# Attention backward: transposes of dS, dK, dV and dQ all by DMA, and twelve products of a pair on GpSimd

## The chip, the cores and the metric

The kernel runs on one core of a Trainium2 chip. The metric is device time in microseconds, the median of three runs. The program orders the instructions of TensorE, SyncE and GpSimd by hand in the part that is changed here; ScalarE and VectorE follow the order of the code's emission through a scheduler. Engines are called PE (TensorE), ACT (ScalarE), DVE (VectorE), POOL (GpSimd) and SP (SyncE) in the profile.

## The reference

One transformer block with adaptive layer norm, forward and backward: sequence 2048, width 512, 32 heads of 16, and a squared-ReLU MLP of width 1792. The result is the block's output and the gradients of its nine differentiable inputs.

```python
def _A_ref(x, wqkv, wo):
    ...
    scores = jnp.einsum('bhqd,bhkd->bhqk', q, k) * scale
    p = _softmax(scores, axis=-1)
    o = jnp.einsum('bhqk,bhkd->bhqd', p, v)
    ...
h = _layernorm(x, axis=-1) * (1 + ca) + sa
x = x + ga * _A_ref(h, A_wqkv, A_wo)
h = _layernorm(x, axis=-1) * (1 + cb) + sb
x = x + gb * _B_ref(h, B_w1, B_b1, B_w2, B_b2)
...
_out, _vjp = jax.vjp(_f, A_x, A_wqkv, A_wo, B_w1, B_b1, B_w2, B_b2, c, w_mod)
_grads = _vjp(grad_out)
```

The change lies in the backward pass of the attention: from stored Q, K, V and dO it makes, for each head, S = QK, P = exp(S), dP = dO V (with the correction term in two extra rows), dS = P * dP, and from these dV, dK (sums over queries) and dQ (a sum over keys).

## The kernel before, in words

The forward pass and the MLP's backward come first (to about 1173 us of the span), then attention backward (`attn_bwd`, to about 2380), then the gradients of the QKV projection.

Attention backward goes over 16 pairs of heads, `(g, jp)`: `g` counts eight groups of four heads, `jp` the two pairs in each. A pair has four chunks `c` of 512 keys and 16 blocks `ib` of 128 queries. Four blocks of queries in one chunk make a group; `m` counts the 16 groups of a pair, `m = 4c + ib // 4`. One step handles one `(c, ib)` for both heads `a` of the pair:

- TensorE makes S into PSUM tile `st` (line 1608), ScalarE its exponential into `pu` (line 1611).
- One step later, TensorE makes dP into PSUM tile `dp` (line 1522), and VectorE multiplies it by `pu` into `ds` (line 1526). For one product of a group, where `off(c, ib)` says so, ScalarE copies dP into SBUF instead (line 1540) and GpSimd multiplies (line 1541). `off` is true in ten of the 16 groups.
- Some steps later, `kv` adds dK and dV of both heads in `acckv` (line 1459); at the end of a chunk ScalarE scales it into `kvT` (line 1462).
- When a group's four steps have their `ds`, SyncE issues one DMA that transposes the group's 32 blocks of 128x128 into a buffer `dsT` (line 1549). Four buffers are called `dsT`; the fifth is the upper half of a large tile `keep` and carries its name in the profile. Where `no_turn` is false (four groups of 16, those with `ib // 4 == 0`), the first four blocks are turned on TensorE (line 1565) and copied by ScalarE (line 1566) instead, and the DMA does the other 28.
- Two groups' buffers together feed the products for dQ into `accq` (`dq`, line 1484), eight batches, two at each even step; the list `pendq` keeps them back until it holds more than eight, so that they run about two groups after the second transpose could be issued. At the end of a pair VectorE scales `accq` into `dqT` (line 1492).

`kvT` and `dqT` have the wrong orientation: heads' dimensions on partitions. They are put into `turnq`, and popped at the fourth step of a group (line 1603): `turn` turns eight blocks of `kvT` on TensorE (line 1472), and ScalarE writes dK and dV from PSUM into `dk_t` and `dv_t` (line 1476); `turn_q` does the same with four blocks of `dqT` (line 1500) and `dq_t` (line 1502). A pair has two turns of `kvT` and one of `dqT`. They borrow the three `st` buffers in PSUM.

GpSimd also issues the loads of the next pair and group of heads, spread over the groups (`pieces`, line 1597), each behind a one-element copy (`tick`, line 1596) that holds it back until the last group's `ds` has begun.

TensorE, SyncE and GpSimd run their instructions in the order of the code; a waiting instruction holds back all behind it on its engine.

Of the kernel before, what the change touches and what calls it, by code (L numbers as in the profile page):

```python
# [9 lines left out]
BF16 = mybir.dt.bfloat16  # L10
# [9 lines left out]
P = 128  # L20
DH = 16
# [84 lines left out]
class K:  # L106
# [1284 lines left out]
    def load_group(self, g):  # L1391
# [5 lines left out]
        if g < 2:  # L1397
            T, o = {}, 0
            for n, e in width.items():
                if g:  # L1400
                    T[n] = qp.tile([P, e], BF16, name=f"{n}g")[:]
                elif n == "K":
                    T[n] = self.keep[:, :e]
                else:
                    T[n] = self.q0[:, o:o + e]
                    o += e
            self.Tq[g] = T
        T, pieces = self.Tq[g % 2], []
        for n, (src, rows) in fm.items():
# [21 lines left out]
    def attn_bwd(self):  # L1431
# [7 lines left out]
        tc, nc = self.tc, self.nc  # L1439
        S, D, H, NQ, ST, SC = self.S, self.D, self.H, self.NQ, self.ST, self.SC  # L1440
        G = 4
        W = 4 * DH
        kvp, stp, dpp = self.kvp, self.stp, self.dpp
# [3 lines left out]
        nc.vector.memset(acckv[:], 0.0)  # L1447
        accq = accp.tile([P, 512], F32, name="accq")
        masked, kvs = self.masked, self.kvs
        pend, pendq, turnq, two = [], [], [], []  # L1450
        own = dT_free[-1]

        def kv(u):
            (T, g, jp, c, ib, kvT, pu, ds) = u
            for j, (n, src) in enumerate((("Q", ds), ("dO", pu))):
                for a in range(2):
                    r = 64 * j + 32 * a
                    col = (2 * jp + a) * DH
                    nc.tensor.matmul(acckv[r:r + DH, :], lhsT=T[n][:, ib, col:col + DH], rhs=src[:, a, :],  # L1459
                                     start=(ib == 0), stop=(ib == ST - 1))  # L1460
            if ib == ST - 1:
                nc.scalar.activation(kvT[:, 512 * c:512 * (c + 1)], acckv[:], ACT.Copy, scale=kvs[:])

        def turn(g, jp, kvT, s0):

            if kvT is None:
                return turn_q(g, jp)
            h0 = 4 * g + 2 * jp
            n = ST // 2
            tp = stp.tile([P, n, P], BF16, name="st")  # L1470
            for st in range(n):
                nc.tensor.transpose(tp[:, st, :], kvT[:, (s0 + st) * P:(s0 + st + 1) * P], self.ident[:])
            v = tp[:].rearrange("p s (t a e) -> p t s a e", t=2, a=2)
            for t, dst in enumerate((self.dk_t, self.dv_t)):
                d = dst[:, s0:s0 + n, h0 * DH:(h0 + 2) * DH].rearrange("p s (a d) -> p s a d", a=2)
                nc.scalar.copy(d, v[:, t, :, :, 0:DH])

        def dq(u):
# [12 lines left out]
            if (c, ib0) == (SC - 1, ST - 2 * G):  # L1491
                nc.vector.tensor_scalar(self.dqT[:], accq[:], self.scale, None, ALU.mult)
                turnq.append((g, jp, None, 0))

        def turn_q(g, jp):

            h0 = 4 * g + 2 * jp
            tp = stp.tile([P, ST // G, P], BF16, name="st")
            for b in range(ST // G):
                nc.tensor.transpose(tp[:, b, :], self.dqT[:, b * P:(b + 1) * P], self.ident[:])  # L1500
            for h in range(2):
                nc.scalar.copy(self.dq_t[:, 8 * h:8 * h + 8, h0 * DH:(h0 + 2) * DH].rearrange("p (s i) e -> p s i e", i=2),
                               tp[:, 2 * h:2 * h + 2, :].rearrange("p i (s e) -> p s i e", s=G))

        def kv_two(n=2):
            for _ in range(n):
                u = pend.pop(0)
                kv(u)
                (T, g, jp, c, ib, kvT, pu, ds) = u
                if ib < ST - 1:  # L1510
                    continue
                if c % 2 and (g, jp) == (NQ - 1, 1):
                    turnq.append((g, jp, kvT, 4 * (c - 1)))
                elif c == SC - 1:
                    turnq.extend((g, jp, kvT, s0) for s0 in (0, ST // 2))

        def dP(u, a):

# [9 lines left out]
        def odd(c, ib):  # L1528
            return (c * SC + ib // G) % 2 == 1

        def no_turn(c, ib):
            return ib // G > 0

        def off(c, ib):
            return odd(c, ib) or (c > 1 and ib // G == 2)

        def dP_pool(u, dp):
            (T, g, jp, c, ib, kvT, pu, dsg, i, grp) = u
            f = (self.junk6, self.csq)[(c * SC + ib // G) % 2]
            nc.scalar.copy(f[:], dp[:])  # L1540
            nc.gpsimd.tensor_tensor(dsg[:, i, 1], f[:], pu[:, 1, :], ALU.mult)  # L1541
# [26 lines left out]
        tick = self.tick  # L1568
        wmt = self.load_wmt()
        T = self.T0  # L1570
        last = None
        for g in range(NQ):
            for jp in range(2):
                if jp == 0:
                    if g + 1 < NQ:
                        Tn, later = self.load_group(g + 1)
                    else:
                        Tn, later = None, self.wq_pieces(1) + wmt[2 * g + 1:]
                    cut = len(later) // 2 if Tn else len(later)
                    pieces = self.pair_pieces(g, 1) + wmt[2 * g:2 * g + 1] + later[:cut]  # L1580
                    later = wmt[2 * g + 1:2 * g + 2] + later[cut:]
                elif g + 1 < NQ:
                    pieces = self.pair_pieces(g + 1, 0) + later
                else:
                    pieces = [(self.xhat1_6[:, st, :], self.xhat1_d.rearrange("(st p) d -> p st d", p=P)[:, st, :])
                              for st in range(ST)]
                kvT = kvp.tile([P, S], BF16, name="kvT")
                end = (g, jp) == (NQ - 1, 1)
                total = len(pieces)
                for c in range(SC):  # L1590
                    c0 = 512 * c
                    for ib0 in range(0, ST, G):
                        m = c * (ST // G) + ib0 // G
                        while pieces and ((total - len(pieces)) * SC * ST <= m * G * total or m == SC * ST // G - 1):
                            if last:
                                nc.gpsimd.tensor_copy(tick[:], last[7][0:1, 0, 0, 0:1])
                            nc.gpsimd.dma_start(*pieces.pop(0))
                        dsg, grp = self.dsp.tile([P, G, 2, 512], BF16, name="ds"), []
                        for i in range(G):
                            ib = ib0 + i  # L1600
                            q = slice(ib * P, (ib + 1) * P)
                            if turnq and i == 3 and m >= (7 if turnq[0][2] is None else 2):
                                turn(*turnq.pop(0))
                            pu = self.pup.tile([P, 2, 512], BF16, name="pu")
                            for a in range(2):
                                stt = stp.tile([P, 512], F32, name="st")
                                rs = slice(64 * jp, 64 * jp + 64)
                                nc.tensor.matmul(stt[:], lhsT=T["QT"][rs, q], rhs=masked["KT"][a][rs, c0:c0 + 512],  # L1608
                                                 start=True, stop=True)
                                held = dP(last, a) if last else None  # L1610
                                nc.scalar.activation(pu[:, a, :], stt[:], ACT.Exp, scale=self.scale)  # L1611
                                if held is not None:
                                    dP_pool(last, held)
                                if a == 0 and i % 2 == 1 and odd(c, ib) and len(pend) >= 4:
                                    kv_two(1)
                            if last:
                                dS(last)
                            last = (T, g, jp, c, ib, kvT, pu, dsg, i, grp)
                            if i % 2 == 1 and len(pend) >= 4:
                                kv_two(1 if odd(c, ib) else 2)  # L1620
                            elif i % 2 == 0 and len(pendq) > 2 * G:
                                for _ in range(4 if end else 2):
                                    dq(pendq.pop(0))
                            if i == 2:
                                turn_ds(dsg, grp, no_turn(c, ib), end and m > 2)
            T = Tn
        with tc.manual_schedule(engines=ALL):
# [23 lines left out]
            self.cs_bc(2)  # L1651
            turn(*turnq.pop(0))
            self.dw_mm(k1, 1, 1, 0, ST)
        assert not turnq and not pend
        self.dw_open = [(1, 0, k0), (2, 0, v0), (1, 1, k1)]

    def dw_mm(self, pt, t, kt, a, b):
# [308 lines left out]
```

## Time and profile before

| | us |
|---|---|
| median of three runs | 2506.41 |
| lowest, highest | 2501.06, 2510.86 |
| the profiled execution, first to last instruction | 2498.5 |
| attention backward in it, from the first transpose of dS | 1173 to about 2380 |

The profiled execution's own time is known only by this span; the median of the runs lies 7.9 us (0.3%) above it.

| engine | busy us in the whole span | share |
|---|---|---|
| PE | 2410.2 | 96% |
| ACT | 2283.1 | 91% |
| DVE | 1695.0 | 68% |
| POOL | 753.5 | 30% |

The shares are averages over parts of the program with different limits: DVE's 68% is made of about three to six tenths in the forward part and over nine tenths in attention backward. DMA transposes are issued on SP's queue (q1 in the profile, 344.68 MB, 1.25 million packets over the whole run), plain loads mostly on POOL's (q0, 104.04 MB). The time of a DMA instruction on SP's queue is that of issuing it; "to landing" is the time from the start of the issue to the completion of its data.

### The profile page before, as it was taken

To read this page: it belongs to the slowest core of one execution; us is meant where nothing else is said; L and a number is where in the kernel's file an instruction comes from. 1 tells how busy PE (TensorE), PEld (TensorE's weight loads), DVE (VectorE), ACT (ScalarE), POOL (GpSimd) and SP (SyncE) were. 2 spreads that over 40 slices of the span, in tenths; PEclk is the share of its full clock that TensorE was granted. 3 is DMA by queue.
4 is the path that set the end of the run, shared out by engine and by line. 5 is a ranking of instruction groups with operands and counts; after the bars stand their busy time and mean duration, and the time that the engine had idled before them with its cause. 6 is when DMAs were issued, how large, how long until landed. Compare 5 with 4: busy or idle time off the path is not lost.

```text
span 2498.5 us, 67897 instructions
## 1 busy us (share of the span) xinstructions
PE 2410.2 (96%) x26211; PEld 1061.6 (42%) x26439; DVE 1695.0 (68%) x3487; ACT 2283.1 (91%) x3757; POOL 753.5 (30%) x1337
## 2 busy tenths in 40 slices
PE   8999999999999999999999999999999999999998
PEld 4555555555555555583233332333333333333343
DVE  6222322422332343576999999999999999999957
ACT  7999999999999997534999999999999999999945
POOL 2344531220131022245222323322333222322223
PEclk9999999999999999999999999999999999999999
DMA  4589661541243045499999999999999999999997
GB/s 166 135 179 208 169 125 47 132 100 40 92 114 98 23 123 147 110 199 216 232 235 233 232 227 231 237 234 231 230 235 239 234 230 236 234 233 236 238 217 192
DMA packets 1293547, 454.13 MB, mean 182 GB/s; under 512 B 1236948, under 2 KB 1261398, under 8 KB 1293222
## 3 DMA queue, kind: packets, MB, share of 16 engines
q1 hardware_dynamic: 1252422, 344.68, 71.8%
q0 software_dynamic: 38720, 104.04, 13.9%
q8 instruction: 207, 3.39, 0.6%
q10 hardware_dynamic: 2080, 1.05, 0.2%
q14 instruction: 118, 0.97, 0.1%
HBM read 75.83 MB, written 64.49 MB: 56 GB/s over the span
## 4 chain that ended last, share of the span: by engine, by line
PE 49%; ACT 35%; DMA 7%; issue 5%; DVE 3%; POOL 1%; SPq 1%; ACTq 0%; DVEq 0%; POOLq 0%
ACT pu L391 26%; PE st L1608 17%; PE acckv L1459 8%; ACT pu L1611 6%; DMA dsT<-ds 5%; PE accq L1484 5%; PE st L388 4%; PE dp L1522 2%; PE accbank L322 2%; PE dps L1050 2%; PE dp L1659 1%; PE st L1754 1%; ACT csq L1540 1%; PE pps L1237 1%; DVE ds L1526 1%
## 5 line engine op out<-in xcount | busy, mean ns | idle before, releaser
L1526 DVE TENSOR_TENSOR ds<-dp,pu 128x512 bf16<-128x512 f32 x1888 | 1166.0, 682 | 34.6 <-PE dp L1522 19.1
L1611 ACT ACTIVATE pu<-st 128x512 bf16<-128x512 f32 x2048 | 1073.8, 666 | 34.7 <-PE st L1608 21.3
L391 ACT ACTIVATE pu<-st 128x1024 bf16<-128x1024 f32 x992 | 912.1, 1077 | 4.2 <-PE st L388 3.7
L388 PE MATMUL st<-QTm,KTq 128*128 128x512 bf16 x1859 | 560.9, 377 | 27.1 <-ACT pu L391 6.1
L322 PEld LDWEIGHTS <-pu 128*128 128x128 bf16 x8192 | 346.7, 96 | 236.1 <-issue 3.0
L1522 PE MATMUL dp<-kvm,q 64*128 64x512 bf16 x1024 | 365.0, 384 | 2.0 <-DVE ds L1526 0.7
L322 PE MATMUL accbank<-Vaug,pu 128*128 128x17 bf16 x8192 | 357.4, 171 | 8.3 <-ACT Vaug L522 1.1
L1522 PE MATMUL dp<-kvm,dOTg 64*128 64x512 bf16 x1024 | 363.6, 383 | 0.3
L1608 PE MATMUL st<-kvm,q 64*128 64x512 bf16 x1024 | 349.4, 382 | 5.4 <-ACT pu L1611 0.2
L1608 PE MATMUL st<-kvm,QTg 64*128 64x512 bf16 x1024 | 348.1, 381 | 6.5
L1541 POOL TENSOR_TENSOR ds<-csq,pu 128x512 bf16<-128x512 f32 x128 | 147.2, 1150 | 627.0 <-ACT csq L1540 553.6
L388 PEld LDWEIGHTS <-KTq 128*128 128x128 bf16 x1984 | 188.4, 96 | 176.9 <-issue 124.8
L1459 PE MATMUL acckv<-ds,Qg 128*16 128x512 bf16 x1024 | 176.2, 382 | 0.3
L1459 PE MATMUL acckv<-pu,q 128*16 128x512 bf16 x1024 | 176.3, 383 | 0.0
L1459 PE MATMUL acckv<-ds,q 128*16 128x512 bf16 x1024 | 176.2, 383 | 0.0
L1459 PE MATMUL acckv<-pu,dOg 128*16 128x512 bf16 x1024 | 176.0, 382 | 0.0
L302 POOL DMA_DIRECT2D QTm<-QTq_d x124 | 63.1, 511 | 341.5 <-PE st L388 320.0
L1608 PEld LDWEIGHTS <-q 64*128 64x128 bf16 x1024 | 67.0, 94 | 163.5 <-issue 150.6
L1608 PEld LDWEIGHTS <-QTg 64*128 64x128 bf16 x1024 | 67.1, 94 | 160.6 <-issue 145.7
L329 DVE RECIPROCAL rl<-accbank 128x4 f32<-128x4 f32 x128 | 22.9, 179 | 158.3 <-PE accbank L322 158.2
L1522 PEld LDWEIGHTS <-q 64*128 64x128 bf16 x1024 | 88.8, 93 | 52.9 <-issue 43.3
L1522 PEld LDWEIGHTS <-dOTg 64*128 64x128 bf16 x1024 | 88.2, 93 | 52.9 <-issue 43.8
(390 smaller groups left out, 3055.1 us busy)
## 6 DMA issues: line engine op xcount, KB each, us to landing
KTq<-KTq_d POOLq DMA_DIRECT2D x24, 512.0 KB, 3.9
duT_d<-auT POOLq DMA_DIRECT2D x3, 1792.0 KB, 7.9
aT_d<-rT POOLq DMA_DIRECT2D x3, 1792.0 KB, 11.5
KTq_d<-KTq SPq DMA_DIRECT2D x32, 128.0 KB, 2.1
QTq_d<-ev_fm SPq DMA_DIRECT2D x32, 128.0 KB, 4.3
ktm_d<-ev_tm POOLq DMA_DIRECT2D x32, 128.0 KB, 2.5
VTq_d<-vT POOLq DMA_DIRECT2D x4, 1024.0 KB, 6.3
dx<-dx_d SPq DMA_DIRECT2D x16, 256.0 KB, 4.6
```

Source lines behind the costliest of these rows:

```text
L302: nc.gpsimd.dma_start(QTm[j][32 * j:32 * j + 32, :], self.QTq_d[g, 32 * j:32 * j + 32, 512 * qc:512 * (qc + 1)])
L322: nc.tensor.matmul(acc[:, a, sub, :], lhsT=pu[:, a, sub * P:(sub + 1) * P], rhs=Vaug[:, kb, h, :], start=(kb == 0 and a == 0 and sub == 0) ...
L388: nc.tensor.matmul(stt[:, a, :], lhsT=KT[:, kb * P:(kb + 1) * P], rhs=QTm[2 * jp + a][:], start=True, stop=True)
L391: nc.scalar.activation(pu[:], stt[:], ACT.Exp, scale=self.scale)
L1050: nc.tensor.matmul(pt[:], lhsT=a[st], rhs=g_tm[:, st, :], start=(st == 0), stop=(st == ST - 1))
L1459: nc.tensor.matmul(acckv[r:r + DH, :], lhsT=T[n][:, ib, col:col + DH], rhs=src[:, a, :], start=(ib == 0), stop=(ib == ST - 1))
L1484: nc.tensor.matmul(accq[r:r + 32, o:o + 256], lhsT=T["K"][:, 4 * c + sub, col:col + 32], rhs=v[:, r // 32 % 2 * 2:r // 32 % 2 * 2 + 2, 4 * ...
L1522: nc.tensor.matmul(dp[:], lhsT=T["dOT"][rd, ib * P:(ib + 1) * P], rhs=masked["VT"][a][rd, 512 * c:512 * (c + 1)], start=True, stop=True)
L1526: nc.vector.tensor_tensor(dsg[:, i, a], dp[:], pu[:, a, :], ALU.mult)
L1541: nc.gpsimd.tensor_tensor(dsg[:, i, 1], f[:], pu[:, 1, :], ALU.mult)
L1608: nc.tensor.matmul(stt[:], lhsT=T["QT"][rs, q], rhs=masked["KT"][a][rs, c0:c0 + 512], start=True, stop=True)
L1611: nc.scalar.activation(pu[:, a, :], stt[:], ACT.Exp, scale=self.scale)
```

## The change

It does five things.

- `no_turn` is true everywhere: the DMA transposes all 32 blocks of dS in each group, and TensorE and ScalarE turn none.
- `off` is true wherever `ib // 4 > 0`: twelve groups of 16 instead of ten hand one product to GpSimd.
- Outside the last pair, what `turnq` holds goes to `cross` instead of `turn`: SyncE issues a DMA that transposes eight blocks of `kvT` (or the four of `dqT`) into a free part of `keep`, and two groups later GpSimd copies from there into `dk_t` and `dv_t` (or `dq_t`), in two instructions of 256 elements a partition.
- `kv_two` puts `kvT` into `turnq` after the second and the fourth chunk of every pair; before, it did so twice after the fourth.
- `kvT` is allocated once for all pairs.

```diff
+        def cross(g, jp, kvT, s0):
+
+            h0 = 4 * g + 2 * jp
+            n = ST // 2
+            tk = self.keep[:, ST * P:(ST + n) * P].rearrange("p (s k) -> p s k", k=P)
+            tq = self.keep[:, (ST + n) * P:(ST + n + ST // G) * P].rearrange("p (s k) -> p s k", k=P)
+            if kvT is None:
+                nc.sync.dma_start_transpose(tq, self.dqT[:])
+
+                def spread():
+                    for h in range(2):
+                        nc.gpsimd.tensor_copy(
+                            self.dq_t[:, 8 * h:8 * h + 8, h0 * DH:(h0 + 2) * DH].rearrange("p (s i) e -> p s i e", i=2),
+                            tq[:, 2 * h:2 * h + 2, :].rearrange("p i (s e) -> p s i e", s=G))
+            else:
+                nc.sync.dma_start_transpose(tk, kvT[:, s0 * P:(s0 + n) * P])
+
+                def spread():
+                    v = tk.rearrange("p s (t a e) -> p t s a e", t=2, a=2)
+                    for t, dst in enumerate((self.dk_t, self.dv_t)):
+                        d = dst[:, s0:s0 + n, h0 * DH:(h0 + 2) * DH].rearrange("p s (a d) -> p s a d", a=2)
+                        nc.gpsimd.tensor_copy(d, v[:, t, :, :, 0:DH])
+            return spread
...
-                if c % 2 and (g, jp) == (NQ - 1, 1):
+                if c % 2:
                     turnq.append((g, jp, kvT, 4 * (c - 1)))
-                elif c == SC - 1:
-                    turnq.extend((g, jp, kvT, s0) for s0 in (0, ST // 2))
...
         def no_turn(c, ib):
+            return True
+
+        def off(c, ib):
             return ib // G > 0
-
-        def off(c, ib):
-            return odd(c, ib) or (c > 1 and ib // G == 2)
...
+        kvT = kvp.tile([P, S], BF16, name="kvT")
...
-                            if turnq and i == 3 and m >= (7 if turnq[0][2] is None else 2):
-                                turn(*turnq.pop(0))
+                            if spreads and i == 3 and m >= spreads[0][0]:
+                                spreads.pop(0)[1]()
+                            if turnq and i == 3 and m % 8 >= (7 if turnq[0][2] is None else 2):
+                                if end:
+                                    turn(*turnq.pop(0))
+                                else:
+                                    spreads.append((m + 2, cross(*turnq.pop(0))))
```

More of the change, by code (lines that the diff above doesn't have):

```diff
@@ L1449, in attn_bwd @@
         masked, kvs = self.masked, self.kvs
-        pend, pendq, turnq, two = [], [], [], []
+        pend, pendq, turnq, spreads, two = [], [], [], [], []
         own = dT_free[-1]
@@ L1586, in attn_bwd @@
                               for st in range(ST)]
-                kvT = kvp.tile([P, S], BF16, name="kvT")
                 end = (g, jp) == (NQ - 1, 1)
@@ L1653, in attn_bwd @@
             self.dw_mm(k1, 1, 1, 0, ST)
-        assert not turnq and not pend
+        assert not turnq and not pend and not spreads
         self.dw_open = [(1, 0, k0), (2, 0, v0), (1, 1, k1)]
```

## The prediction

> **What bounds the kernel now.** I read the page first, for where the change lies and how busy each engine is there.
>
> ```profile
> span 2498.5 us, 67897 instructions
> ...
> DMA  4589661541243045499999999999999999999997
> ...
> PE 49%; ACT 35%; DMA 7%; issue 5%; DVE 3%; POOL 1%; SPq 1%; ACTq 0%; DVEq 0%; POOLq 0%
> ACT pu L391 26%; PE st L1608 17%; PE acckv L1459 8%; ACT pu L1611 6%; DMA dsT<-ds 5%; PE accq L1484 5%; PE st L388 4%; PE dp L1522 2%; PE accbank L322 2%; PE dps L1050 2%; PE dp L1659 1%; PE st L1754 1%; ACT csq L1540 1%; PE pps L1237 1%; DVE ds L1526 1%
> ```
>
> The whole right half of the slices is attention backward, and the DMA engines stand at nine tenths in every slice of it. The chain that ended last goes through the transpose of dS (`dsT<-ds`) for 5% of the span: TensorE has waited for these landings, if only briefly each time. So before I ask what TensorE gains, I ask how full the queue is to which the work goes.
>
> Second, the instructions of line 1549, the transposes by DMA, in a stretch of the steady part. Columns: instructions, then shortest, median and longest in ns, first and last start.
>
> ```profile
> L1549 SPq DMA_TRANSPOSE dsT<-ds x104: 3499/4262/5700, 1554.0 to 2155.1; - x104
> L1549 SPq DMA_TRANSPOSE keep<-ds x25: 3550/4209/5392, 1573.7 to 2136.7; - x25
> ...
>   PE accq L1484: 1.8, 5
> ...
> DMA to landing us min/median/max: 5.1/6.9/8.8
> ```
>
> These are 129 issues, so 128 intervals of one group of rows each, 16 to a pair of heads: eight pairs in 601.1 us, 75.1 us for a pair and 4.70 for a group. SyncE spends 4.26 us (median) of each 4.70 on issuing. The fifth buffer of the ring bears the name `keep`; all else is the same. TensorE waited only 1.8 us in all for landings here: the queue keeps up, just.
>
> Third, the timeline of that queue alone (start, duration, count). I show five of its rows; the one-by-one rows of `keep` run from the first here to the last, 25 of them, and average 4.32, which is 0.11 over their median.
>
> ```profile
> 1573.73 3.75 SPq L1549 DMA_TRANSPOSE keep<-ds  x1
> ...
> 1624.30 20.26 SPq L1549 DMA_TRANSPOSE dsT<-ds  x4
> 1644.66 4.23 SPq L1549 DMA_TRANSPOSE keep<-ds  x1
> 1648.98 19.00 SPq L1549 DMA_TRANSPOSE dsT<-ds  x4
> ...
> 2136.72 3.55 SPq L1549 DMA_TRANSPOSE keep<-ds  x1
> ```
>
> From 1624.30 to 1667.98 stand nine issues, with 0.09 and 0.10 us at the two joints that show: the queue runs all but without rest there. A fair mean of one issue is 4.26 + 0.11 = 4.37 us, with 0.09 behind it, so a pair takes 16 x 4.46 = 71.4 of its 75.1 us. **The slack of the queue is 3.7 us a pair**, 5%.
>
> Fourth, the busy time in the same eight pairs (PE, PEld, DVE, ACT, POOL, then clock, DMA share, GB/s).
>
> ```profile
> 1554.01:2155.09 601.08, 593.77 (x6438) 185.92 (x6436) 587.16 (x953) 596.74 (x1218) 181.32 (x352) 1.00 1.21 234
> ```
>
> TensorE, ScalarE and VectorE are all at 98 to 99%, GpSimd at 30%. Five resources stand within 5% of each other; relief to three is worth what the others leave.
>
> **The change part by part.** First what it takes off. The groups in the same stretch (busy us, mean ns):
>
> ```profile
> L1526 DVE TENSOR_TENSOR ds<-dp,pu 128x512 bf16<-128x512 f32 x945 | 583.2, 682 | 13.9 <-PE dp L1522 5.8 <-ACT pu L1611 1.2 <-ACT dv_t L1476 0.3
> L1541 POOL TENSOR_TENSOR ds<-csq,pu 128x512 bf16<-128x512 f32 x64 | 73.6, 1151 | 307.6 <-ACT csq L1540 262.4 <-DVE ds L1526 45.3
> L1540 ACT COPY csq<-dp 128x512 f32<-128x512 f32 x64 | 42.0, 656 | 0.0
> L1596 POOL COPY tick<-ds 1x1 bf16<-1x1 bf16 x136 | 24.0, 177 | 55.9 <-DVE ds L1526 55.9
> L1566 ACT COPY dsT<-st 128x512 bf16<-128x512 bf16 x25 | 15.1, 604 | 0.0
> L1476 ACT COPY dv_t<-st 128x256 bf16<-128x256 bf16 x16 | 6.4, 398 | 0.0
> L1476 ACT COPY dk_t<-st 128x256 bf16<-128x256 bf16 x16 | 6.2, 389 | 0.2
> L1502 ACT COPY dq_t<-st 128x256 bf16<-128x256 bf16 x16 | 5.5, 412 | 0.0
> ```
>
> ScalarE loses, per pair, four evictions of turned dS (4 x 0.60), four of dK and dV (12.6/8 = 1.6) and two of dQ (5.5/8 = 0.7), and gains two copies of dP (2 x 0.66): 4.7 - 1.3 = 3.4 us less, from 74.6 to 71.2. VectorE loses two products at 583.2/945 = 0.617: 73.4 to 72.2 us.
>
> TensorE's matmuls overlap, so I price its turns by start to next start:
>
> ```profile
> 1583.59 0.40 PE L1500 MATMUL st<-ident,dqT 128*128 128x128 bf16 x4
> ...
> 1583.92 0.39 PE L1608 MATMUL st<-kvm,q 64*128 64x512 bf16 x1
> ...
> 1700.77 0.40 PE L1565 MATMUL st<-ident,ds 128*128 128x128 bf16 x4
> ...
> 1701.10 0.39 PE L1608 MATMUL st<-kvm,QTg 64*128 64x512 bf16 x1
> ...
> 1710.46 0.62 PE L1472 MATMUL st<-ident,kvT 128*128 128x128 bf16 x8
> 1711.02 0.39 PE L1608 MATMUL st<-kvm,QTg 64*128 64x512 bf16 x1
> ```
>
> A turn of four blocks holds TensorE 0.33 us, one of eight 0.56. Per pair that is 4 x 0.33 (dS) + 2 x 0.56 (dK, dV) + 0.33 (dQ) = 2.8 us. If nothing else stood in the way, a pair would go from 75.1 to about 72.4, where VectorE's 72.2 stops it too.
>
> Now what it puts on SyncE's queue. The dS transposes of four groups go from 28 blocks of 128x128 to 32; a group has 31 on average, so a block costs 4.37/31 = 0.141 us, and 16 blocks 2.3 us a pair. Then three new transposes: two of eight blocks (dK with dV), one of four (dQ). Transposes of these sizes stand elsewhere in the trace:
>
> ```profile
> L1332 SPq DMA_TRANSPOSE dOTq<-dOpad x12: 1232/1236/2390, 461.4 to 965.4; - x12
> ...
> L1248 SPq DMA_TRANSPOSE dxT<-dxb x12: 1195/1202/1445, 446.3 to 946.7; - x12
> ...
> L1737 SPq DMA_TRANSPOSE dqT<-dk_t x8: 1232/1325/2972, 2392.8 to 2458.1; - x8
> L1737 SPq DMA_TRANSPOSE dqT<-dv_t x8: 1300/2820/5517, 2394.1 to 2460.3; - x8
> ```
>
> Eight blocks take 1.24 us on a quiet queue, four take 1.20. So the three cost 2 x 1.24 + 1.20 + 3 x 0.09 = 3.9 us. The lower bound is 20 blocks x 0.141 = 2.8 us: what a small issue costs beyond its blocks would then be won back while the DMA engines empty what was pushed before. The upper bound is the crowded row of line 1737, 2.82 for eight: 2 x 2.82 + 1.4 = 7.0. I take 3.3, nearer to the lower rows, since the loads beside them are those of now. Sum for the queue: 71.4 + 2.3 + 3.3 = **77.0 us a pair** (76.5 to 80.7), against 75.1 now and the 72.4 that the engines would like.
>
> What stands behind a late transpose: the accq products of two groups use both landings, two groups after the second issue became possible. That is 9.4 us; a landing takes 6.9 in the median and 8.8 at most. So there are one or two microseconds of lead, and a queue that falls behind for good uses them up within a pair. Then TensorE waits at line 1484 with every later matmul behind it, and ScalarE and VectorE wait for those. The engines' 2.8 us disappear in that wait.
>
> GpSimd gets two more products (2 x 1.15) and six strided copies of 256 elements, not shown before: between 0.18 (the tick) and 1.15 each, 1.1 to 6.9 us a pair. With 22.7 of 75 us busy now, idle time hides either. Each copy is issued two groups after its transpose, about 9.4 us, against a landing of at most 8.8; behind it in GpSimd's queue stand the next product, the ticks and the loads. The crossing itself waits for data that ScalarE and VectorE wrote groups earlier, so it adds no wait ahead of the next dS. I cost these parts at nothing; the cover is GpSimd's idle 70%.
>
> Fifteen of the 16 pairs cross by DMA; the last keeps its turns of dK, dV and dQ and only sends its 16 blocks of dS: about +1 us. Sum: 15 x (77.0 - 75.1) + 1 = 29.5, say +28 us since the first pair has one crossing, not three. Against the profiled execution's 2498.5 that is 2526; against the median of the runs, 2506.4 (7.9 above, 0.3%), **2534 us**. A measurement here tells 0.5%, 12.5 us, from no change.
>
> **The rivals.**
>
> *The queue takes it, and TensorE's relief counts (faster).* For it: the shortest issues of 3.5 us and eight blocks in 1.24 show a queue that can be quicker than its mean. At the rate of the shortest (28 blocks in 3.5 us, so 32 in 4.0) a pair needs 16 x (4.0 + 0.09) + 3.3 = 68.7 us, and that fits. A pair then comes to 72.4: 15 x -2.7 - 1 = -42, 2464 us; half of it gives 2485. It decides wherever the mean issue of 32 blocks stays under about 4.2 us. Against it: the nine issues that ran without rest took 43.7 us, 4.85 each, more than the mean and not less. The Trainium skill (DMA: Bandwidth & Descriptors, Latency and other measured facts) gives 261 GB/s for DMA transposes with a non-contiguous middle dimension; an estimate from that figure, 532 blocks of 32 KiB, is 66.8 us a pair, which would be this rival. The trace's 234 GB/s, loads included, speaks for less.
>
> *Both nearly cancel (no change).* The mean issue drops a little under load, the pair ends at 74.5 to 75.9: 2497 to 2518.
>
> *GpSimd stalls on a copy whose transpose lands late (slower).* If the crossing lands over 9.4 us after its turn in the code, GpSimd's next product waits, the dS group with it. At 1 us for each of 43 crossings on top of my sum: 2577. The landing row speaks against it. That the change does not do what it says I see only in the last pair.
>
> **How the numbers follow.** My forecast has 0.54, the GpSimd stall 0.04, no change 0.20, the gain 0.22. Slower by over 0.5% is then 0.58, the same 0.20, faster 0.22. My forecast's own range goes from 76.3 a pair (2525) to 79.3 (2570); above that lies the crowded price of small transposes. The gain spreads over 2464 to 2494, and about half of it lies under 2480. From 2480 to 2570 leaves out some 0.11 below and 0.08 above.
>
> **What would show it.** Right: on SyncE's queue the issues follow each other with 0.1 us between nearly everywhere, and their sum fills the pair; `PE accq L1484` waits for DMA for tens of microseconds instead of 1.8 in eight pairs; TensorE, ScalarE and VectorE fall to some 93 to 95%; the chain's DMA share grows well past 7%. Wrong: a pair of 72 to 73 us with gaps left on that queue, or issue times of 32 blocks under 4.2 in the mean. GpSimd rows `dk_t`, `dv_t`, `dq_t` that wait for DMA for microseconds would point to the stall.

## The result and the profile after

| | before | changed |
|---|---|---|
| median, us | 2503.73 (4 runs) | 2573.15 (4 runs) |
| lowest, highest | 2500.91, 2510.86 | 2567.05, 2577.82 |
| profiled execution, first to last instruction | 2498.5 | 2565.2 |

A fourth run of the kernel before has joined the three of the table further up. The changed kernel is slower, by a ratio of times of 1.0269 (95% interval 1.0239 to 1.0299): 69 us, where 28 were forecast. The direction and the bound, SyncE's queue, came as predicted; the size did not, and the time lies 3 us above the range.

The page of the changed kernel, the lines that answer to those of before:

```profile
span 2565.2 us, 67032 instructions
...
DMA  4589752450342144899999999999999999999997
...
PE 39%; DMA 28%; ACT 20%; issue 7%; DVE 3%; POOL 2%; SPq 1%; POOLq 0%; DVEq 0%; ACTq 0%
```

DMA's share of the chain that ended last has gone from 7% to 28%, TensorE's from 49% to 39%. The transposes of dS now stand at line 1571, the crossings of `kvT` and `dqT` at 1510 and 1502. In a stretch of eight pairs (instructions; shortest, median, longest in ns):

```profile
L1571 SPq DMA_TRANSPOSE dsT<-ds x102: 3960/4422/6122, 1490.3 to 2112.4; - x102
L1571 SPq DMA_TRANSPOSE keep<-ds x26: 3976/4370/5451, 1485.4 to 2103.7; - x26
...
DMA to landing us min/median/max: 6.4/7.8/9.1
```
```profile
L1510 SPq DMA_TRANSPOSE keep<-kvT x16: 1300/1302/1308, 1495.8 to 2088.3; - x16
```
```profile
L1502 SPq DMA_TRANSPOSE keep<-dqT x8: 1262/1264/1268, 1519.8 to 2072.4; - x8
```

The 128 groups take from 1485.4 to 2117.5 us, 79.0 us a pair. And SyncE's queue in the timeline (start, duration, count):

```profile
1638.43 14.58 SPq L1571 DMA_TRANSPOSE dsT<-ds  x3
1653.06 1.30 SPq L1510 DMA_TRANSPOSE keep<-kvT  x1
1654.47 4.31 SPq L1571 DMA_TRANSPOSE dsT<-ds  x1
1658.89 4.51 SPq L1571 DMA_TRANSPOSE keep<-ds  x1
1663.49 14.37 SPq L1571 DMA_TRANSPOSE dsT<-ds  x3
1677.91 1.26 SPq L1502 DMA_TRANSPOSE keep<-dqT  x1
1679.27 4.51 SPq L1571 DMA_TRANSPOSE dsT<-ds  x1
```

Each row starts 0.05 to 0.11 us after the one ahead of it has ended. In these rows the queue has no rest; over the eight pairs some 0.4 us a pair is left. Summed over the records of these eight pairs, a pair is 72.85 us of dS transposes, 3.87 of crossings and 2.3 of gaps: 79.0. Before, by the same sum, it was 69.8 of transposes and 5.3 of gaps, of which 3.9 were rest.

Who waits, in the same stretch (engine and line waited for, us in all, times, longest), and the engines' busy time:

```profile
PE accq L1484 <- DMA dsT<-ds: 22.3, 25, 1.3
POOL dk_t L1516 <- DMA keep<-kvT: 12.5, 14, 1.9
...
PE accq L1484 <- DMA keep<-ds: 6.5, 8, 1.6
```
```profile
1485.45:2117.55 632.10, 592.37 (x6147) 157.28 (x6144) 581.84 (x937) 590.33 (x1153) 216.27 (x416) 0.99 1.24 237
```

TensorE waits 28.8 us for dS where it was 1.8, and is busy 94% instead of 99%, VectorE 92%, ScalarE 93%. Two things were not in my forecast: GpSimd waits for the crossings of `kvT`, 0.9 us each time, and outside this stretch two of the pairs took 83.7 and 82.1 us.

### The profile page after: what moved, and what is told of

Same layout as the page of the kernel before. It is cut to its first block, busy times and chain, and to the rows that moved or that the text cites. A ratio compares the mean times of both kernels' runs of the same rounds, so it can differ in the third digit from the quotient of the medians.

```text
span 2565.2 us, 67032 instructions
## 1 busy us (share of the span) xinstructions
PE 2426.7 (95%) x25895; PEld 1008.8 (39%) x25895; DVE 1684.7 (66%) x3455; ACT 2270.0 (88%) x3639; POOL 819.5 (32%) x1455
## 3 DMA queue, kind: packets, MB, share of 16 engines
q1 hardware_dynamic: 1323430, 362.51, 74.6%
## 4 chain that ended last, share of the span: by engine, by line
PE 39%; DMA 28%; ACT 20%; issue 7%; DVE 3%; POOL 2%; SPq 1%; POOLq 0%; DVEq 0%; ACTq 0%
DMA dsT<-ds 19%; ACT pu L391 18%; PE st L388 8%; PE st L1635 7%; DMA keep<-ds 6%; PE acckv L1459 4%; PE accbank L322 3%; PE accq L1484 3%; PE dps L1050 2%; PE pps L1237 2%; DVE ds L1548 1%; PE dp L1544 1%; PE st L1781 1%; PE pps L631 1%; DMA dqT<-dq_t 1%
## 5 line engine op out<-in xcount | busy, mean ns | idle before, releaser
L388 PE MATMUL st<-QTm,KTq 128*128 128x512 bf16 x1984 | 587.6, 377 | 19.5 <-ACT pu L391 6.0
L1635 PE MATMUL st<-kvm,QTg 64*128 64x512 bf16 x1024 | 336.0, 386 | 0.7 <-ACT dq_t L1526 0.2
L1635 PE MATMUL st<-kvm,q 64*128 64x512 bf16 x1024 | 335.0, 384 | 0.3 <-ACT pu L1638 0.2
L1563 POOL TENSOR_TENSOR ds<-junk,pu 128x512 bf16<-128x512 f32 x64 | 74.0, 1156 | 221.9 <-ACT junk L1562 217.2
L1484 PE MATMUL accq<-dsT,keep 128*32 128x256 bf16 x1632 | 111.0, 279 | 25.4 <-DMA dsT<-ds 25.0
L1635 PEld LDWEIGHTS <-q 64*128 64x128 bf16 x1024 | 67.1, 94 | 171.2 <-issue 169.8
L1484 PE MATMUL accq<-dsT,Kg 128*32 128x256 bf16 x1696 | 108.4, 280 | 22.9 <-DMA dsT<-ds 22.6
```

The lines of the kernel that those rows point to most:

```text
L388: nc.tensor.matmul(stt[:, a, :], lhsT=KT[:, kb * P:(kb + 1) * P], rhs=QTm[2 * jp + a][:], start=True, stop=True)
L1484: nc.tensor.matmul(accq[r:r + 32, o:o + 256], lhsT=T["K"][:, 4 * c + sub, col:col + 32], rhs=v[:, r // 32 % 2 * 2:r // 32 % 2 * 2 + 2, 4 * ...
```

## The experiments

My theory (1): SyncE's queue of transposes is the bound, and a pair lasts as long as its issues one after the other. The rivals: (2) GpSimd's copies wait for late crossings and hold up its products; (3) TensorE's or ScalarE's own work still decides. The pair times below are medians over the profiled execution. A ratio is to the kernel before, run again beside the experiment; its medians there went from 2509 to 2516 us, so across experiments the ratios compare better than the medians.

### One part at a time

**dS turned in four groups again** (`e1_turn_ds`):

```diff
         def no_turn(c, ib):
-            return True
+            return ib // G > 0
```

> The changed kernel with one part undone: in four of 16 groups TensorE turns the first four blocks of dS again. Theory 1 (SyncE's queue of transposes is the bound: a pair lasts as long as its issues take one after the other): the queue loses 4 x 0.5 us of a pair's 79.1, so 77.1 us a pair and some 2573 - 31 = 2542 us in all, though TensorE and ScalarE get work back. Theory 2 (GpSimd is the bound: its copies wait for late crossings, and its twelve products stand behind them): nothing of that changes, 2567 to 2579. Theory 3 (TensorE's or ScalarE's work is still what counts): slower than 2573 by 4 x 0.33 us a pair, 2593.

2546.44 us, ratio 1.0134 (1.0087 to 1.0180) to the kernel before; 77.5 us a pair. Giving TensorE and ScalarE their work back makes the kernel 27 us faster (34 by the ratios): theory 3 falls.

**dK, dV and dQ turned on TensorE again** (`e2_turn_kv`), in all pairs `turn(*turnq.pop(0))` in place of `cross`:

> The changed kernel with another part undone: dK, dV and dQ are turned on TensorE as before, no crossing and no copy on GpSimd; all of dS by DMA, twelve products on GpSimd. Theory 1: the queue loses 3.9 us of issues and 0.3 of gaps a pair, 79.1 - 4.2 = 74.9 us, which is still the queue: 2510 us (2500 to 2520), no gain over the kernel before. Theory 2: without the copies GpSimd stalls nothing, and the engines' own 75.1 - 1.3 = 73.8 us a pair shows: about 2484. Theory 3: slower than the changed kernel.

2526.42 us, ratio 1.0062 (1.0038 to 1.0086); 75.7 us a pair. Most pairs came near the queue's 74.9, the median 0.8 above it, but two of 80 us and a longer end put the time 16 us above what I expected, outside its range. Theory 2's gain over the kernel before did not come.

**GpSimd's twelve products alone** (`e3_pool12`), on the kernel before:

```diff
-            return odd(c, ib) or (c > 1 and ib // G == 2)
+            return ib // G > 0
```

> The kernel before with one part of the change alone: GpSimd multiplies in twelve groups of 16. Theory 1: SyncE's queue has the same work and the same slack, so the time stays at 2504 within 0.5%; VectorE loses 1.2 us a pair and ScalarE gains 0.9 to 1.3. Theory 2: two more products a pair that end later than VectorE's hold up the transposes: slower by over 0.5%, above 2516.

2508.12 us, ratio 0.9981 (0.9959 to 1.0002): no change, as theory 1 says.

**The twelve products taken back to ten in the changed kernel** (`e9_pool10`, the edit above reversed):

> The changed kernel with GpSimd's products back at ten groups of 16; all transposes and crossings stay. Theory 1: the queue is the same, VectorE has slack, so 2573 within 0.5%. Theory 2: two products a pair less behind the copies, faster by over 0.5%.

2587.53 us, ratio 1.0316 (1.0289 to 1.0343): slower than the changed kernel by 14 us by the medians and 12 by the ratios, whose intervals overlap. Theory 2 is wrong in sign. Theory 1's no change within 0.5% is just at its edge, so the products on GpSimd may help a little under the full queue. Why, I have not settled.

**GpSimd's copies two groups later** (`e8_spread4`, `m + 4` for `m + 2`):

> The changed kernel with GpSimd's copies four groups after their crossing instead of two, so that the crossing has landed long before; nothing else moves. Theory 1 (SyncE's queue): the same queue, the same time, 2573 within 0.5%. Theory 2 (GpSimd's wait for a late crossing, 0.8 us each in the trace, holds up a product and the group behind it): up to 43 x 0.8 = 36 us less, 2537 to 2560.

2573.25 us, ratio 1.0262 (1.0245 to 1.0280): the same. In its trace no copy of `dk_t` waits for a crossing any more: the list of waits under these copies, 12.5 us in the changed kernel, is empty.

```profile
L1516 POOL COPY dk_t<-keep x20: 389/392/402, 1529.5 to 2283.3; 128x256 bf16<-128x256 bf16 x20
its engine sat idle before it (us, times) until:
who waited for it (us, times):
```

The wait that I had missed is real and costs nothing; theory 2 is gone.

### Taking load off the queue

**24 of the 32 blocks** (`e4_fewer_blocks`):

```diff
-            grp.extend((dsT, 0 if skip else 4))
+            grp.extend((dsT, 8))
```

> The changed kernel, but each DMA transposes only 24 of the 32 blocks of dS; the first eight blocks of each buffer are set to zero once and never written, so that part of dQ's sum is left out. All matmuls, products, crossings and copies stay. Theory 1: the queue needs 16 x 3.5 + 3.9 + 2.0 = 62 us a pair and is no longer the bound; a pair falls to what TensorE and VectorE need, 72.4 us, and the time to 2462 (2455 to 2475), under the kernel before: the relief of TensorE is real and was hidden by the queue. Theory 2: GpSimd's copies still wait or its products still hold up the groups: over 2490. If instead another engine had no slack, 2490 to 2504.

2477.2 us, ratio 0.9859 (0.9806 to 0.9913): faster than the kernel before, though 2 us above the range that I had given. The eight pairs from 1551.4 us on, and the transposes of dS (line 1573 there):

```profile
1551.40:2136.10 584.70, 583.79 (x6148) 159.14 (x6144) 576.90 (x937) 580.65 (x1153) 216.42 (x416) 1.00 0.99 199
```
```profile
L1573 SPq DMA_TRANSPOSE dsT<-ds x104: 2888/3135/4525, 1551.4 to 2136.1; - x104
```

A pair takes 73.1 us, with TensorE busy 99.8% of it and ScalarE 99.3%. So the relief of the engines is real, 2 us a pair against the kernel before where I had worked out 2.7, and the full queue hid it.

**28 of the 32 blocks** (`e10_28_blocks`, `grp.extend((dsT, 4))`):

> The changed kernel, but each DMA transposes 28 of the 32 blocks of dS; the first four blocks of each buffer are zeros, so that an eighth of dQ's sum is left out. With 24 blocks a pair took 73.0 us, with 32 blocks 79.0. Theory 1 as I summed it (a pair lasts as long as the fullest of queue and engines, nothing between): the queue needs 16 x 4.0 + 3.9 + 2.0 = 70 us, so the engines' 73.0 stay and the time is that of the run with 24 blocks, 2477 within 0.5%. Theory 1 with a cost of nearness (an issue of the transposes now and then takes a microsecond longer, the landings have one or two us of lead, and at 95% a late one is not made up before the next): 74 to 75.5 a pair, 2493 to 2515.

2507.23 us, ratio 0.9981 (0.9966 to 0.9996); 74.9 us a pair. The transposes of dS, and who waited for them, in eight of its pairs:

```profile
L1573 SPq DMA_TRANSPOSE dsT<-ds x104: 3362/3792/5582, 1562.5 to 2159.7; - x104
...
  PE accq L1486: 10.0, 12
```

By the records the queue needs 63.6 + 3.9 + 2 = 69.5 us, the engines 73.0, and the pair takes 74.9, with TensorE waiting for landings: the time begins to grow before the queue is full. My sum, which took the larger of the two, had no such term.

**No loads in ten pairs** (`e6_no_loads`): `pieces` holds only the weight matrix's one piece for `1 <= g <= 5`.

> The changed kernel, but in ten of the 16 pairs (groups of heads 1 to 5) the loads of the next heads' data are left out, some 16 of 17 a pair, with the ticks before them; the pairs compute with old data. It asks why an issue of 32 blocks takes 4.55 us in the mean when the shortest take 3.97. Theory 1a (each load holds up the transposes on the DMA engines): the issue falls to 4.1 to 4.2 us in these pairs, the queue to 16 x 4.15 + 3.9 + 2.1 = 72.4 us, a pair to 73 to 74, and the time by ten times 5 to 6 us, to 2513 to 2523. Theory 1b (the rate of the transposes themselves, loads or none): the issue stays at 4.5, the pairs at 78 to 79, the time above 2560.

2530.43 us, ratio 1.0096 (1.0077 to 1.0115). The ten pairs took 74.6 to 77.4 us, an issue 4.22 to 4.38 in the mean of a pair against 4.55. Each expectation was half right: sixteen loads cost a pair 3 us of its queue, and the other 0.35 us above the shortest issue is there without them.

### The price of a crossing

**Each crossing twice** (`e11_double_cross`), a second `dma_start_transpose` with the same operands:

> The changed kernel with each crossing issued twice, to the same place. It prices the crossings. Theory 1: the queue is full, so every microsecond of issue counts: three issues of 1.3 us and 0.1 us of gap more in each of 14 pairs, 4.2 x 14 = 58 us, 2631 (2620 to 2640). By the price that I took in the prediction, 3.3 a pair: 2619. If the engines' DMA work alone counted (20 blocks at the rate of a long issue, 0.12 us each): 2.4 x 14 = 34, 2607.

2718.86 us, ratio 1.0820 (1.0792 to 1.0849), far more than any of the three. The queue's timeline shows that I had built in a wait:

```profile
1638.67 1.31 SPq L1511 DMA_TRANSPOSE keep<-kvT  x1
1642.91 1.23 SPq L1512 DMA_TRANSPOSE keep<-kvT  x1
1644.26 10.06 SPq L1573 DMA_TRANSPOSE dsT<-ds  x2
```

The second starts 2.9 us after the first has ended, when the first has landed, for both write the same place. It prices a wait on that queue: some 9 us more of gaps and 3.7 more of issues made a pair 90 us instead of 79.

**One small transpose more behind each crossing, to a free place** (`e14_extra_small`):

```diff
                 nc.sync.dma_start_transpose(tk, kvT[:, s0 * P:(s0 + n) * P])
+                nc.sync.dma_start_transpose(tx, kvT[:, s0 * P:(s0 + 4) * P])
```

> The changed kernel with one more transpose behind each crossing, of four blocks, to a free place that nobody reads, so that nothing waits for it (the run with doubled crossings wrote to the same place twice, and the second waited for the first). Three more issues a pair, 12 more blocks. Theory 1s (SyncE's time of issuing is what runs out): 3 x (1.2 + 0.1) = 3.9 us a pair, 14 pairs, 55 us: 2628 (2615 to 2640). Theory 1d (the DMA engines' time for the blocks is what runs out, some 0.15 us a block with the loads): 12 x 0.15 = 1.8 us a pair, 25 us: 2598 (2590 to 2606).

2635.95 us, ratio 1.0492 (1.0437 to 1.0547), 63 us above the changed kernel by the medians, 56 by the ratios.

```profile
1645.62 1.30 SPq L1512 DMA_TRANSPOSE keep<-kvT  x1
1647.01 1.22 SPq L1513 DMA_TRANSPOSE keep<-kvT  x1
1648.34 18.18 SPq L1574 DMA_TRANSPOSE dsT<-ds  x4
```

Four blocks cost the queue nearly as much as eight, 1.22 us against 1.30. For the small transposes, what runs out is SyncE's time of issuing (theory 1s), not the DMA engines' time for the blocks: over a pair, nothing that a small issue costs is won back. For the long ones these runs do not tell the two apart, since a load beside a long issue makes it longer, too.

### How near the edge the kernel before was

**Two turned groups instead of four** (`e7_two_turns`), on the kernel before:

```diff
         def no_turn(c, ib):
-            return ib // G > 0
+            return ib // G > 0 or c % 2 == 1
```

> The kernel before with a small part of the change: two of the four groups whose first blocks TensorE turned go to the DMA whole, the other two and all turns of dK, dV and dQ stay. Theory 1: the queue gains 2 x 0.5 us a pair, 72.3 of 75.1, still with 2.8 us of slack; TensorE loses 0.66 us and ScalarE 0.9, so a pair takes 74.5 and the time falls by some 9 us, 0.4%, if the landings' lead of one to two us suffices. If that lead is already used up by single slow issues, no gain, or up to 0.3% slower.

2519.22 us, ratio 1.0046 (1.0024 to 1.0069); 76.4 us a pair. One microsecond more on the queue and 0.66 less on TensorE: slower by 0.5%, a little more than the 0.3% that I had allowed for.

**The same with a longer lead** (`e12_lead`: a sixth buffer, `len(pendq) > 3 * G`) **and its twin** (`e13_no_wmt`, the old lead; both without the loads of one matrix):

> The kernel before with two instead of four groups turned in part on TensorE, as in the run with two turns, but with a sixth buffer for the transposed dS and the products of dQ one group later, so that a landing has 4.7 us more of lead. To make room, the 16 loads of one weight matrix are left out and the input's gradient is computed with other data. If single slow issues against a short lead made that run slower than the kernel before (theory 1 with a cost of nearness): a pair of 74.5 us or less, 2490 to 2502, faster than its twin without the lead by 0.6 to 1%. If the mean of the issues made it slower: no difference from the twin.

> The twin of the run with more lead: two groups turned in part on TensorE, the same 16 loads left out, but five buffers and the old lead. By either theory as the run with two turns less the loads' cost, 2519 - 4 = 2515.

2523.8 us, ratio 1.0053 (1.0034 to 1.0072), with the lead; 2514.28, ratio 1.0010 (0.9994 to 1.0026), without. The lead did not help, it cost. The transposes of dS with the lead, and after them those of the twin:

```profile
L1548 SPq DMA_TRANSPOSE dsT<-ds x107: 3640/4512/6427, 1483.1 to 2092.2; - x107
...
  DVE ds L1525: 4.9, 8
```
```profile
L1548 SPq DMA_TRANSPOSE dsT<-ds x102: 3474/4234/6228, 1480.3 to 2078.7; - x102
...
  PE accq L1483: 8.8, 12
```

TensorE no longer waits, VectorE waits for a `ds` buffer to be read instead, and the issues are longer where the queue may run on: 0.28 us in the median of these rows, 0.13 in the mean of the eight pairs. So a longer lead by itself does not mend two turns. That the longer issues are the reason is what these rows suggest, not shown: the `ds` buffers may have become the next limit. Why issues differ in length is the next question.

### Transposes by themselves

Two small programs without any attention (`m1_transposes_alone`, `m2_rest`).

> No attention at all: a small program that only transposes by DMA from SBUF to SBUF, 32 issues in each part, one part after the other, all outputs zero. Parts: 32 blocks an issue without rest; 28; 8; 4; 32 blocks with one load of 64 KB for each; 32 blocks paced by VectorE, so that the queue rests between; 32 blocks with one of 8 after every third. Theory 1s: 32 blocks without rest start every 4.0 to 4.1 us, the shortest issue of the attention kernel, and the paced ones take the same 4.0. Theory 1d (an issue looks shorter when the queue rested, since the engines still work off what was pushed): without rest one starts every 4.3 us or more, above the time of a paced issue, and 8 blocks cost less than 1.3 us of start to start between long ones.

Line 30 is 32 blocks an issue without rest, line 36 eight, line 39 four, line 42 32 blocks with a load for each:

```profile
L30 SPq DMA_TRANSPOSE dst<-src x32: 4782/4924/5054, 9.5 to 163.2; - x32
```
```profile
L36 SPq DMA_TRANSPOSE dst<-src x32: 1232/1334/1343, 313.3 to 356.1; - x32
```
```profile
L39 SPq DMA_TRANSPOSE dst<-src x32: 1190/1264/1265, 360.4 to 400.9; - x32
```
```profile
L42 SPq DMA_TRANSPOSE dst<-src x32: 4726/5094/5411, 404.5 to 564.8; - x32
```

Not 4.0, and hardly less with rest: 4.92 us without, 4.87 paced. A load of 64 KB adds 0.17 to the issue. (The part with small issues between long ones waited for landings, as in the doubled crossings, and tells nothing.)

> Again transposes alone, 24 issues of 32 blocks in each part: without rest; paced by VectorE at two slower rates, so that the queue rests for 2 us and for 5 us; without rest into buffers at other distances in SBUF; without rest beside matmuls; without rest beside elementwise work on VectorE and ScalarE. The first program gave 4.92 us an issue without rest and 4.87 with 0.4 us of rest, the attention kernel 3.97 at the shortest and 4.4 to 4.6 in the mean. If a rest of some microseconds makes an issue shorter, the two slow parts show 4.0 to 4.4. If the place of the buffers decides, the fourth part does. If the engines' work beside it matters, the last two are longer than 4.92. If none of these, all stay at 4.9, and why the attention kernel's are shorter stays open.

Without rest (line 33), and with 6.7 us of rest behind each (line 43):

```profile
L33 SPq DMA_TRANSPOSE dst<-src x24: 4772/4926/5052, 11.1 to 125.3; - x24
```
```profile
L43 SPq DMA_TRANSPOSE dst<-src x24: 4669/4816/4864, 333.8 to 598.5; - x24
```

Rest makes an issue 0.11 us shorter in the median. The other parts, other places in SBUF and other engines' work beside it, had medians of 4.91 to 4.93. Of the 0.18 us between the means of before and after (4.37 and 4.55), the 28 blocks in a quarter of before's issues (3.95 against 4.50 us) give 0.14, and the little that is left would fit the missing rest. Why an issue in the attention kernel is shorter than alone stays open; nothing I varied shows it.

## Why the prediction was right in direction and wrong in size

**What bounds it.** Right. The queue had some 4 us of rest a pair, and the change put more on it than that. The signs that I had named for it came: issues 0.1 us apart, TensorE waiting for tens of microseconds, engines at 92 to 94%, DMA's share of the chain up. So did a sign of the GpSimd stall, copies that wait for DMA, without its cost. Taking blocks off the queue gave a pair of 73.1 us, near the 72.4 that I had given the engines.

**The sum for the queue, 77.0 us a pair: mis-sized.** The step that failed is "The lower bound is 20 blocks x 0.141 = 2.8 us: what a small issue costs beyond its blocks would then be won back", from which I took 3.3 for three crossings, gaps included. They measured 3.87 without gaps, and a pair without any rest has 1.9 us of gaps where I had 1.4 besides: 1.0 more in all. The small extra transposes showed that nothing is won back; the quiet rows, 3.9 with gaps, were the better price. The dS transposes came to 72.85 instead of 72.3, 0.6 more, and 0.4 of rest was left in the queue where my sum had none. Together 2.0 us a pair, 30 us in 15 pairs. Each was small and each went the same way. The nine issues that I had quoted at 4.85 us, gaps included and almost without rest, I used only as an argument against the rival. They pointed upwards, but as a price they go too far: by them alone the sum would have been some 83 us a pair.

**A pair is the larger of queue and engines: too simple.** With 28 blocks a queue of 69.5 us and engines of 73.0 made 74.9, and two turned groups fewer already cost 0.5%. I had no term for nearness. A longer lead did not remove it in the run that tried; more is not settled.

**The last pair and the end.** I gave them 1 us. In the two profiled executions the last pair, up to the first transposes of the next stage, is 2.8 us longer, and the rest of the program 6.6. With the 30 us of the other pairs this makes up nearly all of the 39 us by which the forecast for the profiled execution, 2526, was missed. That end took 105.1 to 105.7 us in the five profiles of the kernel before and its variants, and 105.0 to 113.5 in the ten of the changed kernel and its variants. So the change seems to make a longer end possible; why, I have not shown.

**GpSimd costs nothing.** Right in the price, wrong in the reason: I had held that a crossing lands within 9.4 us of its turn in the code. It lands 3.3 us after its issue begins, but on the full queue the issue comes late, and the copy waits. The wait has no effect, as the later copies showed. The twelve products change nothing in the kernel before and may help by some 12 us in the changed one.

**The rival in which the queue takes it.** It did not come: issues of 32 blocks took 4.55 us in the mean, above its threshold of 4.2. But the threshold was too generous. With 28 blocks the mean issue was 3.97 us and a pair still took 74.9 instead of 72.4; a clear gain came only with 24 blocks, at 3.3 us. The Trainium skill's 261 GB/s for a non-contiguous middle dimension (DMA: Bandwidth & Descriptors, Latency and other measured facts), by which this rival would have won, is not reached here: alone, 32 blocks of 32 KiB start every 4.96 us, 211 GB/s.

## What to carry to other kernels

When a change moves work onto a queue that is 95% busy, count every small issue at its full time with its gap, take the issues that ran without rest as an upper bound, and expect the time to grow before the sum reaches the period. A transpose that is cheap on the engines is not cheap on the issuing queue: four blocks cost 1.26 us there, nearly as much as eight. To find out whether relief elsewhere is real, take load off the queue, even by leaving work out.

## What the runs showed of the hardware that was not expected

- Small DMA transposes from SBUF to SBUF cost nearly the same time of issuing: four blocks of 128x128 take 1.26 us and eight 1.33, where 28 took 4.32 and 32 take 4.92, all alone and without rest.
- The same 32 blocks take 4.92 us alone and 3.96 to 6.1 in the attention kernel, 4.55 in the mean. Rest of the queue, place of the buffers, and work on TensorE, VectorE and ScalarE, tried in the small programs, do not explain it.
- Plain loads beside the transposes lengthen them: without sixteen loads a pair took 3 us less, and alone one load of 64 KB for each issue added 0.17 us to it.
- TensorE's granted clock was clearly lower only in the runs where it was idle longest. In eight steady pairs it was 1.00 in the kernel before (TensorE busy 99%), 0.99 in the changed one (94%), 0.96 with the small extra transposes (91%) and 0.91 with the doubled crossings (87%).
